# Four attention-fed MLPs on one core: three late matmul stages by a seven-product scheme on half tiles

## The chip, the cores and the metric

The kernel runs on 1 core of one Trainium2 chip. The metric is the device time of one execution in microseconds (us). The program is built by a scheduler that reorders the instructions of each engine, so the order on an engine is not the order of the source.

## The reference, cut to what matters

```python
# attention: 4 batches x 12 heads, 448 x 64, float32; all MLP weights float64
q_n, k_n = rmsnorm(q, g_q), rmsnorm(k, g_k)
attn = softmax(scale * q_n @ k_n.T)              # per batch and head
x = (attn @ v)  ->  [1792, 768]                  # 4 batches x 448 tokens
ab = (x @ w_a) * (x @ w_b)                       # w_a, w_b: 768 x 1536
y = ab @ w_out                                   # 1536 x 768
h = y @ w2_in                                    # 768 x 2048
g = max(h, 0) + alpha * min(h, 0)
out = g @ w2_out                                 # 2048 x 768
```

## The kernel before, in words

**Tiles.** A batch b (448 tokens) is one pass through four stages: `a` gives AB[b, 0..11] (gated products), `y` gives Y[b, 0..5], `h` gives G[b, 0..15], `o` gives the output columns. Data lie transposed: 128 features on the partitions, 448 tokens along the free axis. Every float32 value is kept as two float16 values, high and low. A product of one 128x128 weight block with one 128x448 data tile is three matmuls into one PSUM bank (`prod`, L752, `mm`, L107): high by high, high by low, low by high. A *unit* is one weight tile's worth of these: 18 matmuls in `a`, `y` and `h` (six blocks), 12 in `o` (four blocks). A stage `a` has 24 units, `y` 12, `h` 16, `o` 24, that is 432, 216, 288 and 288 matmuls.

**Order.** `stages` (L594) sets the order of the stages, with the attention of later batches put between units at a rate that `RATE` (L920) sets; before `a` of batch b its attention is finished. Attention's PSUM pools (`ps_s`, two tiles of two banks, and `ps_x`, one bank) stay open to the end; the MLP stages use `ps_m` (three banks).

**Weights.** The first use of a weight tile loads it as float64, converts, scales and splits it on ACT and DVE (`w_convert`, `w_scale`, `w_split`), and writes the two float16 halves to HBM scratch (`sc_a`, `sc_y`, `sc_h`, `sc_o`). Every later use loads it from there (`w_load`, L618, DMA L624, on SP's queue) into one of 5 buffers (`wh_p`), asked for 4 units ahead (`AGAIN`, L720). `next_w` (L740) ends a unit: it drops the buffer, asks for loads, and takes one job from the list `tasks`.

**Ends of stages.** `stage_a` leaves AB in float32 (L788, DVE, with the sum of squares by ACT L791), then forms one scale for the batch from all twelve sums (`total` L123, a matmul named `tot` on TensorE, and `power` L110, four small DVE instructions, L797) and splits AB by it (`split`, L764), at once where `y` follows, else one tile a unit by `tasks`. `stage_o` finishes output chain m one chain behind: ACT scales and reorders (L880), TensorE transposes four 128x112 pieces (L887), ACT copies with a scale (L889), a DMA stores (L890).

**The end of a1** is where batch 2's attention, the last AB chain of batch 1 and y1 meet: DVE runs the softmax steps (L417 maximum, L472 and L473 sum and reciprocal, L480 the low half of the probabilities, L531 the low half of x) with the last AB chain (L788).

## Time and profile before

| | us |
|---|---|
| median of 3 runs (lowest, highest) | 1224.51 (1223.84, 1224.89) |
| the profiled execution | 1225.36 |
| its span in the trace | 1223.6 |
| TensorE (PE) busy | 1158.7 (95%) |
| VectorE (DVE) busy | 673.7 (55%) |
| ScalarE (ACT) busy | 714.4 (58%) |

PE's share is an average: in the first 340 us the weights are converted and the attention of batches 0 and 1 runs, and DVE, ACT and the DMA engines are as busy as PE; from a2 on (598 us to the end) DVE is busy for 172 of 626 us, and PE runs almost without a gap. The profile's own time is 0.85 us above the median, and its span is 1.76 us shorter than that time.

### The profile page before, as it was taken

Reading aid. Unit: us, or ns where it says so; the run is one execution under the profiler, and the core shown is the slowest. Engines: PE = TensorE matmul, PEld = TensorE weight load, DVE = VectorE, ACT = ScalarE, POOL = GpSimd, SP = SyncE. Lnnn points to the kernel's source line nnn. Section 1 sums busy time; section 2 is a strip of 40 time slices with the busy share of each in tenths; the row PEclk is TensorE's granted clock in tenths of the full one; section 3 lists DMA queues with packets and bytes.
Section 4 is the critical chain, followed back from the end, with each engine's and each line's share of the span. In section 5 each row is a group of like instructions: output and inputs, shape, how many; then the busy total and the mean of one; then the engine's idle time right before and its main releaser. Section 6 shows DMA issues by size and latency. Waiting matters only on the chain.

```text
span 1223.6 us, 18095 instructions
## 1 busy us (share of the span) xinstructions
PE 1158.7 (95%) x6550; PEld 595.6 (49%) x6550; DVE 673.7 (55%) x1442; ACT 714.4 (58%) x1458; POOL 11.9 (1%) x32
## 2 busy tenths in 40 slices
...
GB/s 186 175 164 217 311 324 324 278 298 301 318 261 300 266 257 246 189 230 177 208 153 126 168 106 168 192 191 163 104 116 116 116 117 107 105 151 128 95 129 88
DMA packets 311241, 234.65 MB, mean 192 GB/s; under 512 B 175440, under 2 KB 284496, under 8 KB 311152
## 3 DMA queue, kind: packets, MB, share of 16 engines
...
q0 software_dynamic: 112, 0.07, 0.1%
...
## 4 chain that ended last, share of the span: by engine, by line
PE 52%; DMA 1%; ACT 1%; DVE 1%; issue 0%; SPq 0%; ACTq 0%
PE p L108 48%; PE s L108 2%; PE x L108 2%; PE p L887 1%; DMA pT<-p 1%; DMA kr<-in_k_dram 0%; ACT t L880 0%; DMA qT<-q 0%; ACT pf L434 0%; ACT p L479 0%; DVE p L480 0%; DVE nm L417 0%; SPq L486 0%; DVE ab L788 0%; ACT x L530 0%
## 5 line engine op out<-in xcount | busy, mean ns | idle before, releaser
L108 PEld LDWEIGHTS <-w 128*128 128x128 f16 x4896 | 474.9, 99 | 466.9 <-issue 39.9
L108 PE MATMUL p<-x,w 128*128 128x448 f16 x1728 | 336.6, 354 | 0.3 <-DVE ab L788 0.2
L108 PE MATMUL p<-g,w 128*128 128x448 f16 x1152 | 228.1, 354 | 6.3 <-ACT g L847 2.2
L108 PE MATMUL p<-y,w 128*128 128x448 f16 x1152 | 222.3, 353 | 0.2 <-DVE t L862 0.2
L108 PE MATMUL p<-ab,w 128*128 128x448 f16 x864 | 169.5, 356 | 1.4 <-ACT ab L766 1.2
L417 DVE TENSOR_REDUCE nm<-s 128x2 f32<-128x896 f32 x84 | 91.2, 1085 | 38.3 <-PE s L108 38.2
L480 DVE SCALAR_TENSOR_TENSOR p<-pf,ri,p 128x448 f16<-128x448 f32 x126 | 84.1, 680 | 30.7 <-ACT p L479 30.5
L479 ACT ACTIVATE p<-pf,ri 128x448 f16<-128x448 f32 x126 | 81.2, 664 | 33.9 <-DMA pT<-p 25.8
L862 DVE SCALAR_TENSOR_TENSOR t<-t,al,p 128x448 f32<-128x448 f32 x55 | 37.3, 678 | 100.6 <-ACT t L861 100.5
L434 ACT ACTIVATE pf<-s,nm,esc 128x448 f32<-128x448 f32 x126 | 90.1, 719 | 1.4
L788 DVE SCALAR_TENSOR_TENSOR ab<-p,inv_a,t 128x448 f32<-128x448 f32 x48 | 32.5, 678 | 100.0 <-PE p L108 99.8
L880 ACT ACTIVATE t<-p,inv_o 128x448 f32<-128x448 f32 x24 | 25.6, 1065 | 81.5 <-PE p L108 81.5
L712 DVE SCALAR_TENSOR_TENSOR w<-wf,sc,w 128x768 f16<-128x768 f32 (+1 forms) x76 | 70.1, 928 | 3.0 <-ACT w L711 2.5
L791 ACT ACTIVATE junk<-ab 128x448 bf16<-128x448 f32 x48 | 27.6, 575 | 70.4 <-DVE ab L788 69.8
L711 ACT ACTIVATE w<-wf,sc 128x768 f16<-128x768 f32 (+1 forms) x76 | 65.5, 869 | 3.4 <-DMA sc_h<-w 1.7
L644 ACT ACTIVATE wf<-raw 128x768 f32<-128x768 f32 (+1 forms) x76 | 63.7, 843 | 4.6 <-DMA raw<-in_moe_w_in_dram 2.7
L650 DVE SCALAR_TENSOR_TENSOR wf<-raw,wf 128x768 int32<-128x768 int32 (+1 forms) x76 | 65.8, 867 | 0.3
L658 ACT ACTIVATE junk<-wf 128x768 bf16<-128x768 f32 (+1 forms) x76 | 59.2, 779 | 1.4 <-DVE wf L650 1.3
L861 ACT ACTIVATE t<-p 128x448 f32<-128x448 f32 x55 | 29.8, 542 | 48.0 <-PE p L108 47.9
L108 PE MATMUL s<-kT,qT 128*64 128x448 f16 x252 | 48.4, 376 | 9.2 <-DMA kT<-k 6.3
L847 ACT ACTIVATE g<-t,cgf 128x448 f16<-128x448 f32 x55 | 36.7, 668 | 34.6 <-DVE t L862 34.6
L848 DVE SCALAR_TENSOR_TENSOR g<-t,cgf,g 128x448 f16<-128x448 f32 x55 | 37.5, 682 | 29.5 <-ACT g L847 29.5
...
## 6 DMA issues: line engine op xcount, KB each, us to landing
w<-sc_a SPq DMA_DIRECT2D x72, 384.0 KB, 3.2
w<-sc_h SPq DMA_DIRECT2D x48, 384.0 KB, 3.1
w<-sc_o SPq DMA_DIRECT2D x72, 256.0 KB, 3.1
w<-sc_y SPq DMA_DIRECT2D x36, 384.0 KB, 3.2
...
```

The source lines that it names most:

```text
L108: nc.tensor.matmul(out=o, lhsT=a, rhs=b, start=first, stop=last)
L417: nc.vector.tensor_reduce(out=nm, in_=ps[:, :, 0:S], axis=AX.X, op=ALU.max, negate=True)
L434: nc.scalar.activation(out=pf, in_=ps[:, j, 0:S], func=AF.Exp, bias=nm[:, j:j + 1], scale=scale[j], accum_out=su[:, j:j + 1],)
L479: nc.scalar.activation(out=t[:, 0, :, 0:KP], in_=pf, func=AF.Copy, scale=r)
L480: nc.vector.scalar_tensor_tensor(out=t[:, 1, :, 0:KP], in0=pf, scalar=r, in1=t[:, 0, :, 0:KP], op0=ALU.mult, op1=ALU.subtract,)
L644: nc.scalar.activation(out=t, in_=hi.bitcast(F32), func=AF.Prelu, scale=2.0 ** -112, alpha=-(2.0 ** 32))
L650: nc.vector.scalar_tensor_tensor(out=ti, in0=lo, scalar=29, in1=ti, op0=ALU.logical_shift_right, op1=ALU.bitwise_or)
L658: nc.scalar.activation(out=junk(768, size(kind)), in_=t, func=AF.Square, accum_out=sums[0][:, j:j + 1])
L711: nc.scalar.activation(out=w[:, 0], in_=t, func=AF.Copy, scale=s)
L712: nc.vector.scalar_tensor_tensor(out=w[:, 1], in0=t, scalar=s, in1=w[:, 0], op0=ALU.mult, op1=ALU.subtract)
L848: nc.vector.scalar_tensor_tensor(out=x[:, 1], in0=t, scalar=cgf[:, f:f + 1], in1=x[:, 0], op0=ALU.mult, op1=ALU.subtract,)
L862: nc.vector.scalar_tensor_tensor(out=t, in0=t, scalar=al[:, f:f + 1], in1=ps, op0=ALU.mult, op1=ALU.add)
```

## The change

`stages` becomes "a0 y0 h0 o0 a1 y1 a2 h1 o1 y2 h2 a3 o2 y3 o2 h3 o3": h2 goes ahead of a3, and o2 is done in two pieces, its first two pairs of output chains ahead of y3 and the third behind it. Stages o2, y3 and o3 (`FAST`) use Strassen's scheme in Winograd's form: for a pair of output chains and for the two halves of the contraction and of the tokens, seven products of half tiles take the place of eight. A product has 128x128 weights and 128x224 data, and is again three matmuls. A pair takes 7 units of 18 matmuls in y (378 in the stage) and 14 units of 12 in o (504 in the stage). What comes with it:

- Four of the seven weight operands are sums of weight blocks (S1 to S4). `form_block` makes them from the scratch: 4 loads, one DVE add of the halves (L679), four DVE sums of a quarter each (L683 to L686), ACT's high half (L690), DVE's low half (L691), 4 stores. There are 12 such blocks for o (1024 elements a partition) and 6 for y (1536). They are written in the source from a2 on, one step a unit, as the list `back`.
- The data operands are sums too: `forms` (DVE L884 to L886 on 448, 224 and 224 elements, ACT L902 and DVE L904 or L906 for the halves, 1568 elements a partition in all) in `stage_h` of batches 2 and 3 and behind a3.
- Seven products of a pair are put together by `gather` (DVE adds out of PSUM, one ACT copy).
- The attention pools are closed ahead of h2, and their room goes to five PSUM banks (`ps_l`) and to the new tiles.
- Weights of fast units come from the scratch or from the formed sums into `wf_p` (6 buffers), still asked for 4 units ahead.
- The batch scale of AB (`scale`) is done at once where y follows, else two units into the next stage. Behind o2's pieces, transposes and stores go into the next stage's units by `tasks`; behind o3 they come one after the other.
- y takes AB's even tiles first, o its weight parts in the order 0, 2, 1, 3, and the powers of two of the scales move (`head`).

```diff
-    stages = "a0 y0 h0 o0 a1 y1 a2 h1 o1 y2 a3 h2 y3 o2 h3 o3".split()
+    stages = "a0 y0 h0 o0 a1 y1 a2 h1 o1 y2 h2 a3 o2 y3 o2 h3 o3".split()
+    FAST = ("o2", "y3", "o3")
+    OPEN = "h2"
+    PIECES = {"o2": [range(2), range(2, 3)]}
...
+    FORMS = (("A11", 0), ("S2", 5), ("S3", 2), ("A22", 6), ("S1", 1), ("S4", 4), ("A12", 3))
...
+    def form_block(kind, i, j, cols):
+        w = cols.stop - cols.start
...
+        def whole():
+            d["r"] = raw().bitcast(F32)[:, 0:4 * w].rearrange("p (q n) -> p q n", q=4)
+            nc.vector.tensor_tensor(d["r"], d["x"][:, :, 0, :], d["x"][:, :, 1, :], op=ALU.add)
+
+        def sums():
+            r = d["r"]
+            nc.vector.tensor_tensor(r[:, 3], r[:, 2], r[:, 3], op=ALU.add)
+            nc.vector.tensor_tensor(r[:, 2], r[:, 0], r[:, 2], op=ALU.subtract)
+            nc.vector.tensor_tensor(r[:, 0], r[:, 3], r[:, 0], op=ALU.subtract)
+            nc.vector.tensor_tensor(r[:, 1], r[:, 1], r[:, 0], op=ALU.subtract)
+
+        def halves():
+            d["o"] = o = raw().bitcast(F16)[:, 0:8 * w].rearrange("p (q l n) -> p q l n", q=4, l=2)
+            nc.scalar.copy(o[:, :, 0, :], d["r"])
+            nc.vector.tensor_tensor(o[:, :, 1, :], d["r"], o[:, :, 0, :], op=ALU.subtract)
+
+        def store():
+            for q, name in enumerate(("S2", "S4", "S3", "S1")):
+                nc.sync.dma_start(out=formed[kind, i, name, j][:, :, cols], in_=d["o"][:, q])
+
+        back.extend((load, whole, sums, halves, store))
...
+        if key[-1] == "s":
+            kind, i, (f, j), _ = key
+            t = wf_p.tile([128, 768], F32, tag="wf", name="ws").bitcast(F16)
+            t = t[:, 0:2 * WIDE[kind]].rearrange("p (l n) -> p l n", l=2)
+            nc.sync.dma_start(out=t, in_=form_source(kind, i, f, j))
+            w16[u] = t
+            return
...
+        elif back and cur[0] > state["back"]:
+            t = back.pop(0)
+            if t:
+                t()
...
+    def forms(r, s, name):
+
+        nc.vector.tensor_tensor(r[:, 1:3], r[:, 2:5:2], r[:, 0:3:2], op=ALU.subtract)
+        nc.vector.tensor_tensor(r[:, 5], r[:, 4], r[:, 1], op=ALU.subtract)
+        nc.vector.tensor_tensor(r[:, 6], r[:, 3], r[:, 5], op=ALU.subtract)
...
+        f = []
+        for j0, j1, x in parts:
+            nc.scalar.activation(out=x[:, 0], in_=r[:, j0:j1], func=AF.Copy, scale=s)
+            if s == 1.0:
+                nc.vector.tensor_tensor(x[:, 1], r[:, j0:j1], x[:, 0], op=ALU.subtract)
...
+    def fast(kind, F, pairs, evac):
...
+            for _ in range(7 * (last + 1)):
+                yield
+                u = cur[0]
+                _, _, (f, j), _ = stream[u]
+                w = unit()
...
+                ps = out[f]
+                for x in range(kk):
+                    hi, lo = w[:, 0, x, :], w[:, 1, x, :]
+                    t = F[j * kk + x][FORMS[f][1]]
+                    mm(ps, hi, t[:, 0], j + x == 0, False)
+                    mm(ps, hi, t[:, 1], False, False)
+                    mm(ps, lo, t[:, 0], False, j == last and x == kk - 1)
+                if j == last:
+                    evac(i, f, ps, None if apart else banks[BANKS[f][0]])
+                next_w()
...
+    def gather(d, f, ps, bank):
...
+        if f == 0:
+            d["p"], d["u"] = pair(), pair()
+            nc.scalar.copy(d["p"][:, 0], ps)
+        elif f == 1:
+            add(d["p"][:, 1], ps, d["p"][:, 0])
+        elif f == 2:
+            add(d["u"][:, 0], ps, d["p"][:, 1])
...
+                x, add_to = 0, d.pop("p")
+            if bank is None:
...
+            else:
+                d[x] = late["t"].tile([128, S], F32, tag="t", name="t2")
+                add(halves_of(d[x]), halves_of(bank[:, 0:S]), add_to)
+            if f == 4:
+                add(d["p"][:, 1], ps, d["p"][:, 1])
...
+    def fast_o(b, pairs):
...
+        d, ready, turned = {}, [], []
+
+        def evac(i, f, ps, bank):
+            if f in (1, 6) and turned:
+                turn_out(b, *turned.pop(0))
+            if f in (0, 5) and ready:
+                m, t, s = ready.pop(0)
+                turned.append((m, turn_in(t, s)))
+            gather(d, f, ps, bank)
+            for j, at in ((1, 4), (0, 6)):
+                if f == at:
+                    m = 2 * i + j
+                    ready.append((m, d.pop(j), inv["o"][:, m:m + 1]))
+
...
+        else:
+            for m, t, s in ready:
+                tasks[0:0] = [
+                    lambda t=t, s=s: turned.append(turn_in(t, s)),
+                    lambda m=m: turn_out(b, m, turned.pop(0)),
+                ]
...
-        power(total(ssab[:, b % 2], KF), sab[:, b:b + 1], iab[:, b:b + 1])
+
+        def scale():
+            power(total(ssab[:, b % 2], KF), sab[:, b:b + 1], iab[:, b:b + 1], 2)
+
+        now = stages_after("a", b) == "y"
+        after(now, lambda f: f and f(), [scale] if now else [None, scale])
...
+        def pair(i):
+            r, at = blocks()
+            for j in range(2):
+                nc.scalar.copy(at[j], halves_of(raw.pop(2 * i + j)))
+            AB[b, i] = forms(r, sab[:, b:b + 1], f"ab{b}_{i}")
+
+        if f"y{b}" in FAST:
+            for i in range(KF // 2):
+                tasks.extend((lambda i=i: pair(i), None, None, None))
...
+            if f"o{b}" in FAST:
+                i, j = f // 2, f % 2
+                if j == 0:
+                    rs[i] = blocks()
+                nc.scalar.activation(
+                    out=rs[i][1][j], in_=halves_of(t), func=AF.Copy, scale=cgf[:, f:f + 1]
+                )
+                if j == 1:
+                    G[b, i] = forms(rs.pop(i)[0], 1.0, f"g{b}_{i}")
+                return
...
+            if st == "a2":
+                for kind in "oy":
+                    for x in range(CHAINS[kind][0] // 2):
+                        form_weights(kind, x)
+                state["back"] = cur[0]
+            if st == OPEN:
...
+                att_ctx.close()
+                late["ps"] = ctx.enter_context(
+                    tc.tile_pool(name="ps_l", bufs=5, space=bass.MemoryType.PSUM)
+                )
+                late["f"] = ctx.enter_context(tc.tile_pool(name="lf", bufs=8))
+                late["q"] = ctx.enter_context(tc.tile_pool(name="lq", bufs=3))
+                late["t"] = ctx.enter_context(tc.tile_pool(name="lt", bufs=4))
```

On **DVE at the end of a1** stood, before (x_3 is a tile of batch 2's attention, `ab_1_11` the last AB chain of batch 1):

```order
L480 SCALAR_TENSOR_TENSOR p_2_110<-pf,ri,p_2_110 128x4x112
L417 TENSOR_REDUCE nm<-s 128x2
L480 SCALAR_TENSOR_TENSOR p_3_111<-pf,ri,p_3_111 128x4x112
L472 TENSOR_SCALAR su<-su 128x2
L473 RECIPROCAL ri<-su 128x2
L531 SCALAR_TENSOR_TENSOR x_3_6390<-x,x_3_6390 128x448
L386 SCALAR_TENSOR_TENSOR v_6745<-vr,sx,v_6745 112x8x64
L480 SCALAR_TENSOR_TENSOR p_0_108<-pf,ri,p_0_108 128x4x112
L788 SCALAR_TENSOR_TENSOR ab_1_11_6414<-p,inv_a,t 128x448
```

and now (line numbers are the changed kernel's, so L480 is L484, L472 is L476, L531 is L535 and L788 is L1051; `raw` is a tile of `form_block`):

```order
L679 TENSOR_TENSOR raw<-raw 128x1024
L476 TENSOR_SCALAR su<-su 128x2
L683 TENSOR_TENSOR raw<-raw 128x256
L477 RECIPROCAL ri<-su 128x2
L684 TENSOR_TENSOR raw<-raw 128x256
L685 TENSOR_TENSOR raw<-raw 128x256
L686 TENSOR_TENSOR raw<-raw 128x256
L691 TENSOR_TENSOR raw<-raw 128x4x256
L535 SCALAR_TENSOR_TENSOR x_3_6393<-x,x_3_6393 128x448
L390 SCALAR_TENSOR_TENSOR v_6748<-vr,sx,v_6748 112x8x64
L484 SCALAR_TENSOR_TENSOR p_0_111<-pf,ri,p_0_111 128x4x112
L1051 SCALAR_TENSOR_TENSOR ab_1_11_6417<-p,inv_a,t 128x448
```

The third of the weight blocks that the scheduler has brought forward into a1 stands between p_3 and x_3; two more are earlier in a1, three in y1, and six of o's with one of y's in a2; the rest of y's are in h2 and a3.

On **PE at the start of h1** (`w_7695` is the weight tile of its first unit before, `w_7840` and `w_7867` those of its second and third now, `tot<-ssab` the sum for AB's scale of batch 2) stood, before:

```order
L108 LDWEIGHTS w_7695
L108 MATMUL p<-y_3_6849,w_7695 128x448
L108 MATMUL tot<-ssab,ones 128x12
L108 LDWEIGHTS w_7695
L108 MATMUL p<-y_3_6849,w_7695 128x448
```

and now:

```order
L110 LDWEIGHTS w_7840
L110 MATMUL p<-y_5_7055,w_7840 128x448
L110 MATMUL tot<-ssab,ones 128x12
L110 LDWEIGHTS w_7867
L110 MATMUL p<-y_0_6546,w_7867 128x448
```

The matmul for the scale has moved from the middle of the first unit to the boundary of the second and third.

On **ACT at the end of the program** (`t` scaled chains of o3, `ob` the copies that are stored, `q_..<-l` the first product of the last pair) stood, before:

```order
L880 ACTIVATE t_12022<-p_11942,inv_o_139 128x7x64
L889 ACTIVATE ob_12029<-p_12024,cum_135 112x512
L880 ACTIVATE t_12089<-p_12009,inv_o_139 128x7x64
L889 ACTIVATE ob_12096<-p_12091,cum_135 112x512
L880 ACTIVATE t_12135<-p_12076,inv_o_139 128x7x64
L889 ACTIVATE ob_12142<-p_12137,cum_135 112x512
```

and now:

```order
L1167 ACTIVATE t_13243<-t2_13212,inv_o_142 128x7x64
L963 COPY q_13245<-l_13216 128x224
L1180 ACTIVATE ob_13282<-p_13277,cum_138 112x512
L1167 ACTIVATE t_13403<-t2_13373,inv_o_142 128x7x64
L1180 ACTIVATE ob_13434<-p_13429,cum_138 112x512
L1167 ACTIVATE t_13439<-t2_13437,inv_o_142 128x7x64
L1180 ACTIVATE ob_13446<-p_13441,cum_138 112x512
```

Before, `t` and `ob` take turns, chain by chain, with a chain of matmuls between them; now the last two `t` stand behind the last pair's products, with one `ob` between them, and on PE the last eight transposes stand together at the end.

## Rows read from the trace of the kernel before

**Rows 1.** The page's section 1, PE: busy time, share of the span, instructions.

```profile
PE 1158.7 (95%) x6550; PEld 595.6 (49%) x6550; DVE 673.7 (55%) x1442; ACT 714.4 (58%) x1458; POOL 11.9 (1%) x32
```

**Rows 2.** Stage windows of PE (o0, y1, y3, o3): length, busy (instructions), clock, DMA share, GB/s.

```profile
338.00:431.70 93.70, 78.38 (x463) 0.98 1.09 273
...
547.20:597.70 50.50, 50.50 (x301) 0.99 0.81 189
...
1006.70:1047.60 40.90, 40.90 (x218) 1.00 0.35 103
...
1160.50:1223.60 63.10, 57.52 (x314) 0.98 0.38 106
```

**Rows 3.** PE's waits: 600 to 760 us, from 1000 us, 538 to 548 us.

```profile
PE tot L108 <- ACT junk L791: 1.8, 1, 1.8
...
PE p L887 <- ACT t L880: 2.3, 2, 1.1
...
PE tot L108 <- ACT junk L791: 3.3, 1, 3.3
```

**Rows 4.** The timeline's end: start, length, engine, line, operation, tiles, [idle before, releaser].

```profile
1209.96 0.60 PE L887 MATMUL p<-ident,t 128*112 128x128 f32 x4
...
1210.40 6.97 PE L108 MATMUL p<-g,w 128*128 128x448 f16 x36
...
1217.41 1.06 ACT L880 ACTIVATE t<-p,inv_o 128x448 f32<-128x448 f32 x1 [6.07 <-PE p L108]
...
1218.52 0.65 PE L887 MATMUL p<-ident,t 128*112 128x128 f32 x4 [1.15 <-ACT t L880]
1219.26 0.69 ACT L889 ACTIVATE ob<-p,cum 112x512 f32<-112x512 f32 x1 [0.79 <-PE p L887]
```

**Rows 5.** Groups by shape, PE's weight loads: busy, mean ns, idle before, releaser.

```profile
L108 PEld LDWEIGHTS <-w 128*128 128x128 f16 x4896 | 474.9, 99 | 466.9 <-issue 39.9 <-ACT w L711 3.9 <-DVE w L712 1.3
...
L887 PEld LDWEIGHTS p<-ident,t 128*112 128x112 f32 x96 | 11.2, 134 | 10.6 <-ACT t L880 8.0
```

**Rows 6.** Groups by shape, DVE and ACT durations of 448 to 768 elements.

```profile
L711 ACT ACTIVATE w<-wf,sc 128x768 f16<-128x768 f32 x52 | 48.9, 942 | 3.4 <-DMA sc_h<-w 1.7 <-PE p L108 1.5
...
L711 ACT ACTIVATE w<-wf,sc 128x512 f16<-128x512 f32 x24 | 16.6, 713 | 0.0
...
L352 DVE TENSOR_TENSOR k<-kr,k 112x512 f16<-112x512 f32 x18 | 12.3, 684 | 1.1 <-ACT k L343 1.1
...
L326 DVE TENSOR_TENSOR qr<-qr,r 128x448 f32<-128x448 f32 x18 | 11.2, 620 | 0.1
```

**Rows 7.** DVE's timeline at a1's end and, last, at y1's end.

```profile
539.14 0.17 DVE L472 TENSOR_SCALAR su<-su 128x2 f32<-128x2 f32 x1 [1.33 <-ACT pf L434]
...
540.10 0.62 DVE L531 SCALAR_TENSOR_TENSOR x<-x,x 128x448 f16<-128x448 f32 x1 [0.59 <-ACT x L530]
...
541.97 0.68 DVE L788 SCALAR_TENSOR_TENSOR ab<-p,inv_a,t 128x448 f32<-128x448 f32 x1
...
596.77 0.62 DVE L531 SCALAR_TENSOR_TENSOR x<-x,x 128x448 f16<-128x448 f32 x1
```

**Rows 8.** Stage windows of DVE (y1, h2), columns as in rows 2.

```profile
547.20:597.70 50.50, 37.03 (x80) 0.99 0.81 189
...
951.90:1006.70 54.80, 28.92 (x47) 1.00 0.39 116
```

**Rows 9.** DMA view: queue share and issues in o1, then in 220 to 330 us.

```profile
q1 hardware_dynamic: 26129, 13.02, 75.4%
...
w<-sc_o SPq DMA_DIRECT2D x21, 256.0 KB, 3.2
...
sc_h<-w SPq DMA_DIRECT2D x14, 384.0 KB, 7.5
```

**Rows 10.** The view of tile w on SP's queue, from 950 us to the end.

```profile
DMA to landing us min/median/max: 2.8/3.0/4.8
```

More of the change, by code (lines that the diff above doesn't have):

```diff
@@ new lines, in units_of, with chains, form_source @@
+    def units_of(st, i):
+        if st[0] == "y":
+            return [(f, 0) for f in range(7)]
+        if st == "o3" and i == 0:
+            return [(f, j) for j in range(2) for f in range(7)]
+        return [(f, j) for f in range(7) for j in range(2)]
+    WIDE = {"y": 768, "o": 512}
+    def chains(kind, i):
+        return (2 * i, 2 * i + 1)
+    def form_source(kind, i, f, j):
+        name = FORMS[f][0]
+        if name[0] == "S":
+            return formed[kind, i, name, j]
+        n = chains(kind, i)[int(name[1]) - 1]
+        two = int(name[2]) - 1
+        return scratch[kind, n, two if kind == "y" else 2 * two + j]
@@ L702, in junk @@
     def junk(width, n):
[L703 removed]
+        return jk_p.tile([128, width], BF16, tag="junk", name="junk")[:, 0:n]
     def w_split(u):
@@ L722, in attention_gated_mlps_kernel @@
     seen = set()
-    firsts = [u for u, key in enumerate(stream) if not (key in seen or seen.add(key))]
+    firsts = [u for u, key in enumerate(stream) if key[-1] != "s" and not (key in seen or seen.add(key))]
     again = sorted(set(range(len(stream))) - set(firsts))
@@ L806, in stages_after, with after @@
         return stages[i + 1][0] if i + 1 < len(stages) and stages[i + 1][1] == str(b) else ""
-    def after(now, one, n):
+    def after(now, one, each):
         if now:
-            for i in range(n):
+            for i in each:
                 one(i)
         else:
-            tasks.extend((lambda i=i: one(i)) for i in range(n))
+            tasks.extend((lambda i=i: one(i)) for i in each)
     def stage_y(b):
```

257 lines of the change are left out of this document (195 added, 62 removed).

## The prediction, made before the changed kernel ran

> **What bounds the kernel now.** I read the page's busy times first, then the windows of the stages, then PE's waits, then the timelines at the places that the change touches. PE is busy for 95% of the span [rows 1]; the windows show where the rest is. The stages that change, y3 and o3, run at full clock with PE busy for 40.90 of 40.90 and 57.52 of 63.10 us, the latter cut only by the tail [rows 2]; the DMA engines have a share of 0.35 to 0.38 there. So late in the program the time is the number of matmuls by their pitch: y3 is 12 units of 18, 40.90 / 216 = 189.4 ns for a matmul of 448 columns. Early it is otherwise: o0 has 15.3 us without PE in 93.70, at a DMA share of 1.09. The change takes matmuls out where only PE counts, and puts DVE and DMA work (the weight sums) into a1, y1 and a2, where the attention of the next batch is also on DVE. The first is the gain, the second the price.
>
> **The change part by part.** All is set against the profiled execution, 1225.36 us.
>
> *The products.* y3, o2 and o3 have 216 + 288 + 288 = 792 matmuls of 448 columns now: 792 x 189.4 = 150.0 us. Afterwards there are 378 + 504 + 504 = 1386 of 224 columns. No matmul of 224 columns of this kind stands in the trace, so I bound it. At 2.4 GHz, the level of these stages [rows 2], 448 columns are 186.7 ns, and 2.7 of the 189.4 are left over. From below: half of all, 94.7 ns, 131.3 us, -18.7. From above: the four transposes of 128 columns, whose next matmul starts 0.44 us after the first of them [rows 4], 110 ns each, 152.5 us, +2.5. I take 93.3 + 2.7 = 96.0 ns, 133.1 us, **-16.9**: the left-over once per matmul, near the lower end, because a 448-column matmul is the same instruction with the same weight load, while the transposes are of f32 with loads of 134 ns against 99 ns [rows 5]. That 99 ns is itself longer than 96.0, and could be the new floor: 1386 x 99 = 137.2, -12.8; I hold it for a record that overlaps its neighbours, but it belongs in the range.
>
> The Trainium skill, page "TensorE: Matmul & The Clock Gate", section "LDWEIGHTS (loading the stationary operand)", gives a weight load the time of its columns over 1.2, in ns; for 128 columns that is 107 ns (an estimate from that page), and if the load then set the pitch, 1386 of them would be 148.3 us and the gain 1.7 instead of 16.9. The f16 loads of this trace are recorded at 99 ns, 7% shorter, so it is too slow for this case as it stands; that loads bound the pitch at all is rival C.
>
> *The wait for AB's scale.* PE stands 1.8 us in h1's first unit for the sum of squares that ACT has yet to end [rows 3]. `tot` now stands two units on, over 6 us later: **-1.8** (between that and 0). At a1's end, where y1 follows at once, the like wait of 3.3 us stays.
>
> *Ends of o2 and o3.* Both wait for L880 ahead of the last transposes, 2.3 us together [rows 3]. Behind o2 the transposes now go into units of the next stage, so half of it goes: **-1.1** (to 0). At the very end it gets longer. Now the last matmul is followed by ACT's scaling (1.06), the transposes, ACT's copy (0.69) and the store [rows 4]. Afterwards a DVE addition of 448 elements out of PSUM (0.62 by the like row [rows 6], and some 0.06 of hand-over) comes first, and the copy and transposes of two chains share the end, of which up to 0.69 + 0.5 us can show: I take **+1.2** (0.7 to 1.9).
>
> *The weight sums: their size.* DVE takes 172 ns + 1.0 ns an element (620 at 448, 684 at 512) and ACT 713 ns at 512 and 0.894 more an element [rows 6]. A block for o is 1.2 (1024) + 4 x 0.43 (256) + 1.2 = 4.1 us of DVE, 1.17 of ACT; for y (1536 and 384) 5.6 of DVE. The scheduler puts three into a1, three into y1, seven into a2, five later.
>
> *At a1's end.* The third block stands on DVE between p_3 and x_3, ahead of the last AB chain, whose sum of squares y1's start waits for. DVE idles there for 1.33 us until 539.14 and 0.59 until 540.10 [rows 7]. The first addition (1.2) fits into the first gap. Then come the four sums, 1.72 us, to about 541.15 with the two small softmax steps between; then ACT's half, 1.17 and a hand-over, to 542.4; then DVE's half, 1.2, to 543.7; then x (0.62), v, p and ab as before (ab began 1.87 after x [rows 7]), so that ab ends near 546.3 instead of 542.65: **+3.6**. It is on the path, for all of y1 needs that scale, and PE was already waiting for it. From 0 (other work of PE moves into it) to 5 (a late load too).
>
> *In y1.* Three blocks, 12.3 us, into a stage where DVE is idle for 50.50 - 37.03 = 13.5 us [rows 8], in pieces. The chain that matters is batch 2's attention: its last tile ends at 597.39 [rows 7], and a2's first unit (from 597.70) needs it after 15 of 18 matmuls, 2.8 us on: 3.1 us to spare. If all fits, 0; if nothing fits, 12.3 - 3.1 = 9.2. I take one block of the three as not fitting, 4.1 - 3.1 = **+1.0**, near the lower end, because PE waits for nothing in y1 now (50.50 of 50.50 [rows 2]).
>
> *At nothing.* In a2 seven blocks (30 us) and in h2 the data sums and two y blocks come to a DVE with room: h2 has 28.9 us of 54.8 now [rows 8], and gets 8 x 1.8 (0.62 + 0.40 + 0.40 + 1.74 less two splits of 0.68) + 2 x 5.6 = 25.6 more, 54.5 in all, just full; but PE waits only for the emptying of PSUM, which stands ahead of the sums, and o2 comes a whole a3 later. If that cover is gone, the excess is at most the last pair, 3 us. In o3 the first pair's units go by the first half of the contraction, so that late G sums are hidden behind seven units of 1.15 us. Weight loads: a fast unit of o has 12 x 96.0 = 1.15 us, 256 KB for it; with 6 buffers a load is asked for five units ahead, 5.75 us, against 3.2 us to landing at a queue share of 75% [rows 9] and 4.8 at the worst late in the program [rows 10].
>
> *The sum:* -16.9 - 1.8 - 1.1 + 1.2 + 3.6 + 1.0 = -14.0; 1225.36 - 14.0 = 1211.36. The profiled execution lies 0.85 above the median, so 1210.5 on the median.
>
> **The rivals.**
>
> *A, the forecast:* 1210.5, by itself 1207 to 1214.5 (the upper end has the pitch of 99 ns).
>
> *B, the early losses are hidden:* other work slides into a1's end and the y1 blocks fit. Without 3.6 and 1.0: 1205.9. For it speaks that y1 has as much idle DVE time as the blocks want; against it that the third block stands ahead of the awaited chain in DVE's own order.
>
> *C, slower: the pitch does not halve.* A half tile needs a weight load for half as many columns; if loads of 128 columns, not columns of data, set the pace, there are 594 more of them than before. The other terms sum to +2.9, so it decides from (150.0 - 2.9) / 1386 = 106.1 ns on. At the 110 ns of the transposes [rows 4]: +2.5 + 2.9 = +5.4, 1229.9. Against it: the f16 load's 99 ns [rows 5] is below 106.1; for it: that no matmul under 448 columns shows in these stages.
>
> *D, the attention slips in y1:* DVE and DMA so full that PE has gaps as in o0, 15.3 of 93.70 or 16% [rows 2]; 16% of y1 is 8.2 us instead of 1.0: 1217.7. For it: a1 and o0 run at a DMA share around 1, and the blocks add loads and stores to them. Against it: PE's full y1.
>
> *E, late weights:* landing takes over 5.75 less 0.5 of issue, about 5.2 us. At the 7.5 us of a full queue [rows 9] a unit would last (7.5 + 0.5 + 1.15) / 6 = 1.53 us instead of 1.15, and over the 84 units of o2 and o3 that is +32: 1242. Against it: o1's 3.2 us.
>
> **How the numbers follow.** A 0.58, B 0.15, D 0.13, C 0.08, E 0.04, and 0.02 for more of a1's loss than D has, still under the time before. A measurement of this kernel can tell about 0.2% (2.4 us) from no change. A, B, D and the remainder are faster by more than that: 0.88. C spreads around its break-even: half of it, 0.04, is the same, the other half with E slower, 0.08. The range holds A, B and D and the 99 ns: 1205 to 1219; C and E are left out.
>
> **What would show it.** Matmuls of 128x224 that follow each other by 96 ns in o2, y3 and o3 (99 or 107 to 110 would be C); PE's wait for `tot` at a1's end at about 7 us instead of 3.3, and none in h1; waits of PE for x or for probabilities at y1's end and in a2 below 2 us (over 7 is D); L959's last addition, then L1167, eight transposes and one L1180 behind the last product, some 1.2 us longer than now; w's landing near 3.2 us in o2 and o3 (over 5.2 is E); DVE nearly full in h2 with PE not waiting. The forecast is wrong above all if the pitch is not 96: each ns on it is 1.39 us.

## The result

The changed kernel takes 1239.14 us (median of 4 runs, 1231.94 to 1240.62) against 1224.7 for the kernel before: 1.0103 times its time, 95% interval 1.0078 to 1.0129. It is slower by about 14 us; 1210.5 was forecast, and the range ended at 1219. The profiled execution is one of 1237.92 us, its span 1236.0.

The stages of the changed kernel, PE's windows (start and end in us; then length, busy (instructions), granted clock, DMA share, GB/s), that answer to [rows 2]:

```profile
434.70:559.00 124.30, 110.33 (x660) 0.95 1.05 245
559.00:610.90 51.90, 51.90 (x300) 0.96 0.91 225
610.90:713.30 102.40, 92.50 (x490) 0.97 0.83 220
...
893.30:954.10 60.80, 55.21 (x290) 1.00 0.55 170
...
1036.60:1080.00 43.40, 43.40 (x453) 1.00 0.83 251
...
1178.40:1236.00 57.60, 51.26 (x529) 0.97 0.64 189
```

These are a1, y1, a2, h2, the first half of the stretch of o2 and y3, and o3. The windows of a1, a2 and h2 before, columns as above:

```profile
431.70:547.20 115.50, 110.33 (x660) 0.98 1.00 231
...
597.70:686.20 88.50, 88.27 (x489) 1.00 0.58 151
...
951.90:1006.70 54.80, 54.77 (x291) 1.00 0.39 116
```

The late stages do what was meant: o2, y3 and o3 together take 144.5 us instead of 162.3. The loss is early: a1 124.2 us (115.5 before), a2 102.4 (88.5), h2 60.9 (54.9). Of a2's 13.9 us, 9.7 are time in which PE runs no matmul (9.9 us now, 0.2 before); the other 4.2 are busy time, in a stage whose granted clock is 0.97 instead of 1.00.

The fast stages' matmuls in PE's timeline, and the end of the program, that answers to [rows 4]:

```profile
1053.28 4.76 PE L110 MATMUL l<-g,ws 128*128 128x224 f16 x48
```

```profile
1221.80 6.78 PE L110 MATMUL l<-g,ws 128*128 128x224 f16 x69
...
1228.61 0.62 DVE L959 TENSOR_TENSOR t<-l,q 128x448 f32<-128x448 f32 x1 [3.68 <-PE l L110]
...
1230.82 0.65 PE L1178 MATMUL p<-ident,t 128*112 128x128 f32 x4 [1.81 <-ACT t L1167]
1231.56 0.69 ACT L1180 ACTIVATE ob<-p,cum 112x512 f32<-112x512 f32 x1 [0.79 <-ACT t L1167]
```

48 matmuls in 4.76 us, the last of them recorded with 0.26: 4.50 / 47 = 95.7 ns each, as forecast (96.0). From the last product's end to the span's end it is 7.4 us, 6.2 before: +1.2, as forecast.

What a2 waits for. First SP's queue (total, times, longest), before and after:

```profile
SPq L624 <- PE p L108: 53.3, 18, 4.0
```

```profile
SPq L695 <- DVE raw L691: 10.9, 5, 6.5
SPq L726 <- PE p L110: 7.5, 4, 4.2
```

Before, SP stood idle for 53 of 88.5 us until PE gave a weight buffer back; it was ahead of its work. Now that slack is 7.5 us, and SP stands 10.9 us before the store of a weight sum (L695) that DVE has not finished (L691), with the next loads behind it. Added up over the DMAs that it issues, SP is busy for some 73 of 102.4 us in a2 (27 of 88.5 before) and for some 106 of 124.2 in a1 (87 of 115.5); a load or store of a block takes about 0.6 us of it (median 0.61 in a2), eight a block. One such place, from all engines' timeline:

```profile
694.49 0.66 SPq L675 DMA_DIRECT2D raw<-sc_y  x1
695.25 0.55 SPq L726 DMA_DIRECT2D w<-sc_a  x1
695.89 1.28 SPq L355 DMA_TRANSPOSE qT<-q  x1
...
698.81 1.76 DVE L679 TENSOR_TENSOR raw<-raw 128x1536 f32<-128x1536 f16 x1 [5.88 <-DMA raw<-sc_y]
...
701.67 0.68 DVE L1051 SCALAR_TENSOR_TENSOR ab<-p,inv_a,t 128x448 f32<-128x448 f32 x1
...
702.40 2.15 PE L110 MATMUL p<-x,w 128*128 128x448 f16 x7 [3.45 <-DVE ab L1051]
```

The last load of a block of y is issued at 694.49, 6.0 us behind the third one, with four stores of another block between them. DVE waits 5.88 us for it, and everything that DVE has to do behind it waits too, among it L1051, which empties the PSUM bank that PE wants: PE stands 3.45 us. A gap of 2.75 us at 639.58 comes by a longer way: the load of k for the attention is issued at 633.59, behind a block's stores and the attention's transposes; ACT waits 5.4 us for it, DVE's L240 5.9 us for ACT, and L1051 stands behind L240. In h2 the instruction that empties PSUM is L1150. It stands on DVE behind the additions of y's two blocks and of the data sums, and is PE's only wait there (`PE p L110 <- DVE t L1150`, 5.6 us in 5 pieces); the data sums alone cost nothing in h2 (54.5 us in e2 below). At a1's end the wait for `tot` is 6.8 us instead of 3.3 [rows 3].

### The profile page after: what moved, and what is told of

Same layout as the page of the kernel before. It is cut to its first block, busy times and chain, and to the rows that moved or that the text cites. A ratio compares the mean times of both kernels' runs of the same rounds, so it can differ in the third digit from the quotient of the medians.

```text
span 1236.0 us, 19915 instructions
## 1 busy us (share of the span) xinstructions
PE 1148.2 (93%) x7144; PEld 652.2 (53%) x7144; DVE 810.9 (66%) x1659; ACT 767.7 (62%) x1525; POOL 12.4 (1%) x32
## 5 line engine op out<-in xcount | busy, mean ns | idle before, releaser
L110 PEld LDWEIGHTS <-w 128*128 128x128 f16 x4104 | 399.4, 99 | 415.8 <-issue 63.5
L110 PE MATMUL p<-x,w 128*128 128x448 f16 x1728 | 340.1, 356 | 12.9 <-DVE ab L1051 6.1
L110 PE MATMUL p<-y,w 128*128 128x448 f16 x1152 | 222.3, 352 | 6.4 <-DVE t L1150 6.4
L110 PEld LDWEIGHTS <-ws 128*128 128x128 f16 x1386 | 132.9, 98 | 0.5
L110 PE MATMUL p<-ab,w 128*128 128x448 f16 x648 | 131.9, 364 | 1.2 <-ACT ab L874 1.2
L110 PE MATMUL p<-g,w 128*128 128x448 f16 x576 | 118.3, 359 | 4.6 <-ACT g L1135 3.5
L421 DVE TENSOR_REDUCE nm<-s 128x2 f32<-128x896 f32 x84 | 91.2, 1086 | 27.3 <-PE s L110 27.2
L484 DVE SCALAR_TENSOR_TENSOR p<-pf,ri,p 128x448 f16<-128x448 f32 x126 | 84.1, 680 | 30.7 <-ACT p L483 30.6
L110 PE MATMUL l<-g,ws 128*128 128x224 f16 x960 | 93.8, 259 | 0.0
L438 ACT ACTIVATE pf<-s,nm,esc 128x448 f32<-128x448 f32 x126 | 90.3, 722 | 1.4
L1054 ACT ACTIVATE junk<-ab 128x448 bf16<-128x448 f32 x48 | 27.8, 579 | 57.2 <-DVE ab L1051 57.2
L110 PE MATMUL s<-kT,qT 128*64 128x448 f16 x252 | 48.5, 376 | 11.3 <-DMA kT<-k 6.0
L1051 DVE SCALAR_TENSOR_TENSOR ab<-p,inv_a,t 128x448 f32<-128x448 f32 x48 | 32.5, 677 | 37.4 <-PE p L110 37.4
L110 PE MATMUL s<-kT,qS 128*64 128x448 f16 x252 | 46.9, 366 | 2.6 <-DMA qS<-qT 2.6
L110 PE MATMUL s<-early 128*128 128x448 f32 x84 | 39.7, 599 | 9.9 <-ACT pf L438 9.3
L1150 DVE SCALAR_TENSOR_TENSOR t<-t,al,p 128x448 f32<-128x448 f32 x55 | 36.6, 676 | 15.5 <-ACT t L1149 15.5
```

Of the source, the lines that this page charges most:

```text
L110: nc.tensor.matmul(out=o, lhsT=a, rhs=b, start=first, stop=last)
L421: nc.vector.tensor_reduce(out=nm, in_=ps[:, :, 0:S], axis=AX.X, op=ALU.max, negate=True)
L438: nc.scalar.activation(out=pf, in_=ps[:, j, 0:S], func=AF.Exp, bias=nm[:, j:j + 1], scale=scale[j], accum_out=su[:, j:j + 1],)
L484: nc.vector.scalar_tensor_tensor(out=t[:, 1, :, 0:KP], in0=pf, scalar=r, in1=t[:, 0, :, 0:KP], op0=ALU.mult, op1=ALU.subtract,)
L1051: nc.vector.scalar_tensor_tensor(out=ab, in0=ps, scalar=i, in1=t, op0=ALU.mult, op1=ALU.mult)
L1150: nc.vector.scalar_tensor_tensor(out=t, in0=t, scalar=al[:, f:f + 1], in1=ps, op0=ALU.mult, op1=ALU.add)
```

## The experiments

18 kernels. Ratios are to the kernel before, run beside each, with 95% intervals. The table has the stages of each profiled execution, in us, from a stage's first matmul to the next stage's; o0 and a1 differ by several us between kernels that have the same work there, the others hardly.

| kernel | us | o0 | a1 | y1 | a2 | o1 | y2 | h2 | a3 | o2+y3 | o3 |
|---|---|---|---|---|---|---|---|---|---|---|---|
| before | 1224.7 | 93.7 | 115.5 | 50.5 | 88.5 | 71.4 | 46.9 | 54.9 | 81.7 | 99.3 | 63.0 |
| the change | 1239.1 | 95.9 | 124.2 | 51.9 | 102.4 | 71.1 | 46.8 | 60.9 | 82.3 | 86.9 | 57.6 |
| e1 sums late | 1236.2 | 98.5 | 118.4 | 52.0 | 88.1 | 90.3 | 55.8 | 54.5 | 82.0 | 86.9 | 57.6 |
| e2 no sums | 1210.1 | 97.7 | 118.8 | 52.1 | 88.1 | 71.5 | 46.8 | 54.5 | 81.7 | 86.9 | 57.6 |
| e3 plain order | 1230.7 | 96.1 | 116.4 | 51.0 | 88.8 | 71.7 | 46.9 | 54.5 | 85.2 | 100.8 | 63.1 |
| e4 sums pinned | 1234.4 | 97.3 | 119.8 | 51.1 | 97.5 | 83.2 | 47.8 | 55.0 | 82.5 | 86.9 | 57.6 |
| e5 GpSimd's queue | 1230.4 | 102.3 | 117.8 | 50.9 | 88.1 | 84.9 | 47.6 | 54.5 | 84.2 | 86.9 | 57.6 |
| e6 math only | 1216.7 | 97.7 | 119.4 | 50.7 | 88.7 | 78.2 | 46.8 | 54.5 | 81.7 | 86.9 | 57.9 |
| e7 DMAs only | 1242.8 | 96.4 | 134.4 | 51.4 | 88.5 | 89.3 | 46.8 | 54.5 | 82.0 | 86.9 | 57.6 |
| e8 all in a3 | 1271.1 | 95.0 | 118.7 | 50.8 | 88.5 | 71.6 | 46.8 | 54.5 | 84.6 | 146.1 | 57.7 |
| e9 spread | 1240.5 | 96.0 | 118.6 | 51.6 | 88.2 | 71.4 | 46.8 | 54.5 | 90.4 | 106.8 | 58.1 |
| e10 y3 and o3 | 1227.3 | 99.9 | 120.3 | 50.6 | 88.1 | 71.2 | 46.8 | 57.0 | 84.0 | 98.6 | 57.6 |
| e11 tiny DMAs | 1236.6 | 95.5 | 130.3 | 50.6 | 88.1 | 85.7 | 46.8 | 54.5 | 81.7 | 86.9 | 57.6 |
| e12 plain, G's order | 1231.6 | 100.7 | 114.8 | 51.6 | 88.1 | 71.9 | 46.8 | 54.5 | 85.2 | 101.1 | 63.1 |
| e13 y3 alone | 1225.0 | 96.7 | 120.8 | 51.8 | 88.2 | 71.4 | 46.8 | 54.6 | 81.8 | 94.7 | 62.9 |
| e14 two DMAs | 1228.8 | 95.2 | 119.8 | 51.7 | 88.9 | 89.2 | 47.8 | 54.5 | 81.7 | 86.9 | 57.8 |
| e15 two DMAs, spread | 1212.8 | 97.2 | 117.1 | 50.7 | 88.2 | 71.3 | 46.8 | 54.5 | 81.7 | 92.7 | 57.4 |
| e16 loads ahead | 1227.3 | 99.7 | 120.1 | 51.4 | 88.8 | 85.8 | 46.9 | 54.5 | 81.7 | 86.9 | 57.4 |
| e17 e15, loads ahead | 1217.2 | 95.6 | 119.7 | 50.9 | 88.7 | 71.2 | 46.8 | 54.5 | 81.7 | 92.6 | 57.4 |
| e18 only two DMAs | 1232.7 | 96.0 | 128.8 | 54.0 | 96.4 | 71.4 | 46.8 | 56.6 | 81.7 | 86.9 | 57.5 |

### Which part of the change costs it: e1 to e4

e1 writes the sums later and pins their first DVE addition to its place in the program; e4 only pins it.

```diff
-            nc.vector.tensor_tensor(d["r"], d["x"][:, :, 0, :], d["x"][:, :, 1, :], op=ALU.add)
+            tc.keep_in_program_order(
+                nc.vector.tensor_tensor(d["r"], d["x"][:, :, 0, :], d["x"][:, :, 1, :], op=ALU.add)
+            )
...
-            if st == "a2":
-                for kind in "oy":
+            for kind in [k for k, at_ in (("o", "o1"), ("y", "a3")) if st == at_]:
```

> The whole change, with the weight sums moved: those for o are written from o1 on and those for y from a3 on, two steps a unit, and the first DVE addition of each block keeps its place in the program, so that no block stands on DVE before h1's end and at most one in h2. Theory (the early place of the sums on DVE costs a1, a2 and h2 about 29 us together): a1, y1, a2 and h2 fall back to their times before, 115.5, 50.5, 88.5 and 55, the late gain of 18 us stays: 1204 to 1211 us. Rival 1 (the new stage order and the pools closed early cost it): h2 and a2 stay long, 1225 or more. Rival 2 (the 35 MB of added DMA traffic costs it wherever it runs): 1225 or more, the loss now in o1, y2 and a3.

Measured 1236.24, 1.0089 (1.0064 to 1.0115). a2 and h2 fall back as expected (a1 only to 118.4), but o1 and y2, where eleven of o's twelve blocks now stand beside batch 3's attention, take 27.8 us more than without sums (e2); a3 takes y's six blocks for nothing. The loss moved with the blocks: not the early place as such, but, so far, the company of attention.

e2 leaves the blocks out; a sum's unit reads a scratch tile:

```diff
-        if name[0] == "S":
-            return formed[kind, i, name, j]
-        n = chains(kind, i)[int(name[1]) - 1]
+        n = chains(kind, i)[int(name[1]) % 2 if name[0] == "S" else int(name[1]) - 1]
...
```

> The changed kernel without the weight sums: the blocks are left out, and the fast units read a weight tile of the scratch in the place of each sum. Theory: all of the early loss is the blocks, 1203 to 1209 us, a1 115.5, a2 88.5, h2 near 55. Rival 1 (stage order and pools): 1220 or more, a2 and h2 still long. Rival 2 (DMA traffic of the blocks): as the theory here, told apart by the run with late sums.

1210.11, 0.9873 (0.9844 to 0.9903), just above what was expected, with a1 at 118.8 instead of 115.5. So the blocks cost the change 29 us, and without them the rest is a gain of 15.6 us.

e3 has no fast stage (`FAST = ()`), no blocks, o2 in one piece behind y3.

> The changed kernel with no fast stage and no sums: products as before, but the new order (h2 ahead of a3), the pools closed at h2, the scale of AB two units late, the parts of y and o in the new order. Theory: nothing of the loss is here, 1221 to 1225 us (the kernel before less up to 3 us of waits). Rival 1: 1230 to 1240 us.

1230.68, 1.0041 (1.0022 to 1.006): 5 us slower than before, outside what was expected. a3 (+3.5) and o2 with y3 (+1.5) are peculiar to it and to e12; o0 and a1 are longer in nearly the whole family of kernels made from the change (below).

> The changed kernel with one edit: the first DVE addition of each weight block keeps its place in the program, so that none stands in a1, one at y1's end, five in a2 and h1, six in o1, the others in y2, h2 and a3. Theory: a1 and y1 fall back by 8 to 10 us, a2 by 3 to 8, h2 stays long or gets longer since one more of y's blocks is there: 1220 to 1230 us. Rival 1 and rival 2 (stage order, DMA traffic): as the changed kernel, 1235 to 1241 us.

1234.43, 1.0073 (1.0046 to 1.01), beyond the theory's end: a2 falls back by 5 us and h2 by 6 (h2 was expected to stay long), but o1, which has five of the blocks now, takes 83.2. As in e1, the loss goes where blocks meet attention.

### What of a block costs it: e5 to e7, e11

All four are e1 with something taken away; e7 and e11 pin a block's first store in place of its first addition.

e5: `nc.sync.dma_start` becomes `nc.gpsimd.dma_start` in a block's load and store.

> The kernel with late sums (o's in o1 and y2, y's in a3), but the loads and stores of the blocks are issued by GpSimd, whose queue is nearly empty, not by SP. In the run with late sums o1 took 90.3 us and y2 55.8, without sums 71.5 and 46.9; SP was issuing for 81 of 90 us there, against 39 of 71 before. Theory (the blocks' eight DMAs each, some 0.63 us of issue apiece, fill SP's queue, and the transposes and loads of the attention behind them come late): o1 under 77, y2 under 50, in all 1210 to 1218 us. Rival D (DVE's work and its order): o1 85 or more, 1230 to 1238. Rival B (the DMA engines' bandwidth, share 0.90 in that stage): likewise 1230 or more.

1230.4, 1.0039 (1.001 to 1.0068). y2 falls back (47.6), o1 only from 90.3 to 84.9: half of the 27.8 us goes with the issues off SP's queue, with the same DVE work and about the same bytes (20.2 MB in o1, 20.7 in e1). That lies between the theory (o1 under 77) and its rivals. The edit isn't a clean one: from GpSimd the bytes go in fewer packets (28936 in o1, 41164 in e1). The Trainium skill, page "DMA: Bandwidth & Descriptors", section "Rules for kernel authors", says that spreading DMAs over the issuing engines doesn't help bandwidth and only saves the sequencer's issue time. That agrees with this run: 13.6 us come back though the DMA share of o1 rises, 0.90 to 0.95.

e6: no loads, no stores, the arithmetic on a tile that is set once.

> The kernel with late sums, its blocks without their loads and stores: the same DVE and ACT instructions on a tile that is set once, at the same places; the fast units read scratch tiles in the place of the sums. Theory (SP's queue): o1 71 to 77 us, y2 47 to 49, 1209 to 1216 in all. Rival D (DVE's work): o1 83 or more, 1225 or more.

1216.69, 0.9937 (0.9908 to 0.9966): o1 78.2 (71 to 77 was expected), 6.7 us over e2's; y2 loses nothing.

e7: the loads and stores alone.

```diff
         def whole():
-            d["r"] = raw().bitcast(F32)[:, 0:4 * w].rearrange("p (q n) -> p q n", q=4)
-            nc.vector.tensor_tensor(d["r"], d["x"][:, :, 0, :], d["x"][:, :, 1, :], op=ALU.add)
+            d["o"] = d["x"]
...
+        halves = sums
```

> The kernel with late sums, its blocks without arithmetic: the four loads and the four stores of each stay on SP's queue, the store takes the loaded tile as it is, so the values of the sums are left out. Theory (SP's queue): most of the loss of o1 and y2 stays, o1 83 or more, y2 51 or more, 1224 to 1236 us. Rival D (DVE's work): o1 under 76, 1208 to 1216 us. Rival B (bandwidth): as the theory here; told apart by the run with GpSimd's queue.

1242.79, 1.0137 (1.0103 to 1.0171): o1 89.3, nearly all of e1's loss there, without an instruction on DVE. The scheduler also brought five blocks' loads into a1, and a1 grew to 134.4; y2, which has few of the DMAs left, takes 46.8 where 51 or more was expected.

e11 is e7 with 8 columns a block: `cols = slice(cols.start, cols.start + 8)`.

> The run with the blocks' DMAs alone, each DMA cut to 8 columns of its block (4 KB instead of 128 or 192 KB), as many DMAs at the same places of SP's order; no arithmetic, the fast units read scratch tiles. In the run with full DMAs a1 took 134.4 us and o1 89.3; without sums 118.8 and 71.5. Theory (SP's issue of eight DMAs a block): a1 128 or more, o1 83 or more. Rival B (bytes through the DMA engines): a1 under 121, o1 under 75.

1236.63, 1.0107 (1.0077 to 1.0137): a1 130.3 and o1 85.7. With a thirty-second of the bytes, 11.5 of 15.6 us stay in a1 and 14.2 of 17.8 in o1 (over e2). Neither the bytes nor the number of packets explains it: e11's o1 has 40102 packets, as many as e7's (39440), and the queue's share of the DMA engines is 75.8%, as without sums (76.2% in e2). SP waits 1.0 us in it for the blocks' landings and issues for 73 of 85.7 us (39 of 71.5 in e2): what is left is the issues. How they reach PE, in e1's o1 (window, then ACT's and PE's waits, then the timeline):

```profile
753.40:843.70 90.30, 74.87 (x426) 0.94 0.90 229
```

```profile
ACT p L483 <- DMA pT<-p: 18.4, 6, 8.2
...
PE p L1179 <- ACT t L1168: 15.1, 5, 5.8
```

```profile
764.53 2.59 SPq L697 DMA_DIRECT2D f_o_S<-raw  x4
...
784.60 4.49 SPq L490 DMA_TRANSPOSE pT<-p  x3
...
788.60 0.67 ACT L483 ACTIVATE p<-pf,ri 128x448 f16<-128x448 f32 x1 [8.25 <-DMA pT<-p]
789.17 0.67 ACT L1181 ACTIVATE ob<-p,cum 112x512 f32<-112x512 f32 x1
```

The four stores of a block hold SP for 2.59 us. SP issues for 81 of the 90 us (38 of 71 before, added up as above), so the attention's transposes (pT, in order on the same queue) go out late; ACT's next softmax step waits 8.25 us for one, o's output steps (L1168, L1181) stand behind it on ACT, and PE waits 15.1 us for those. By ACT's order, two of these five waits of PE (10.1 us) follow on late transposes and two others (4.7 us) on a softmax maximum (L421) that DVE gave late. From issue to landing pT takes 3.8 us, 3.5 before: the time is lost ahead of the issue, not on the way.

### Where the sums could go: e8 to e10

e8: all blocks from a3 on, four steps a unit. e9: from h2 on, one step a unit, two in a3. e10: only y3 and o3 fast, in the order of before.

> The changed kernel with all weight sums in a3 and the start of o2, where no attention runs: four steps a unit from a3 on, o's first two pairs, y's, o's third pair, the first DVE addition of each block pinned. DVE has 74 of 82 us free there, SP 74. Theory: nothing waits for SP's queue there but weight loads that are asked for four units ahead; a3 82 to 86 us, 1207 to 1214 in all, the fastest of the correct versions. Rival D (DVE's work): a3 88 or more, for its emptying of PSUM stands behind blocks of 4 to 5.6 us; 1216 to 1225. Rival B: a3 85 or more as well, at a DMA share near 1.

1271.09, 1.0376 (1.0342 to 1.041). No attention runs there, yet the stage overflows: o2 and y3 take 146.1 us, with one gap of PE of 17.7 us before y3. PE waits there for y3's data (L903 on ACT), which stand behind the last three blocks, of o, on DVE and ACT. The last two of these begin 10.8 us apart on DVE: a block in that row lasts as long as its chain of load, additions, store and the next block's load behind that store on SP.

> The whole change, its weight sums spread over the stages in which no attention runs: one step a unit in h2, two in a3, one in o2, in the order o's first two pairs, y's, o's third pair; the first DVE addition of each block pinned. Three blocks stand in h2, eleven in a3, four in o2. Theory (the sums cost where they share SP's queue and DVE with the attention, and are nearly free elsewhere as long as a stage has room for them): a1, y1, a2, o1 and y2 as without sums (a2 88, o1 71.5, y2 47), h2 54 to 58, a3 82 to 85, o2 and y3 together 87 to 92 (86.9 in the changed kernel): 1211 to 1219 us. Rival (a block costs 2 us wherever it is, attention or not): 1240 or more. Against both: if the stages run out of room as in the run with all sums in a3, o2's weights come late again and o2 is longer than 60.

1240.53, 1.0122 (1.0096 to 1.0149): a1 to h2 as without sums, so the place is right, but a3, with nine blocks' additions, loses 8.7 us, and o2 with y3, with six, loses 19.9. PE's waits from a3 to y3:

```profile
PE p L110 <- DVE ab L1054: 6.6, 2, 4.4
PE p L110 <- ACT junk L1057: 5.1, 1, 5.1
PE l L110 <- DMA ws<-f_o_S: 4.5, 2, 2.3
```

The theory that blocks are free away from attention, as long as a stage has room on DVE, falls with these two: before, DVE is busy for 8 of 82 us in a3.

> Only y3 and o3 by seven products, o2 as before, the stages in the order of before, the pools closed at a3; y's sums in a3 (two steps a unit), o's in the rest of a3, h2, y3 and o2 (one a unit). Theory: no block meets the attention of a batch, and the matmuls of y3 and o3 fall from 504 of 448 columns to 882 of 224: 95.4 - 84.1 = 11.3 us of them, 2 lost again at the end and at edges: a3 82 to 83, h2 55 to 57, y3 36 to 37, o3 57.6; 1211 to 1217 us. Rival (2 us a block wherever it is): 1235 or more.

1227.27, 1.0013 (0.9992 to 1.0033): no difference. o3 is 5.4 shorter, but o2 with y3 only 0.7, h2 and a3 are 4.4 longer, and o0 and a1 11 longer.

### The number of DMAs: e14 to e18

e14 is e1 with the four weight tiles of a pair in one HBM tile, and the four sums in one, so that a block has one load and one store of the same bytes:

```diff
-                nc.sync.dma_start(out=x[:, q], in_=s)
+            nc.sync.dma_start(out=x, in_=quad[kind, i, j][:, :, :, cols])
...
+            nc.sync.dma_start(out=sums_of[kind, i, j][:, :, :, cols], in_=d["o"])
```

> The run with late sums (o's in o1 and y2, y's in a3) with one DMA for the four loads of a block and one for the four stores: the four weight tiles of a pair lie in one HBM tile, so do the four sums; the same bytes and pieces, a quarter of the issues. In the run with late sums o1 took 90.3 and y2 55.8, SP issuing for 81 of 90 us. Theory (SP's time goes by the number of DMAs): SP 50 us or less in o1, o1 78 to 82 (DVE's part, 6.7, stays), y2 47 to 49: 1218 to 1226. Rival S (SP's time goes by the pieces of a DMA): an issue lasts 2 us and more, o1 86 or more, 1230 to 1238. Rival B (bytes): likewise 1230 or more.

1228.77, 1.0022 (1.0006 to 1.0037). An issue of four times the bytes lasts about as long in o1 as one of the small ones (median 0.57 us, 0.54 to 0.97), and SP issues for 58 of 89 us instead of 81 of 90. That is less of a fall than the number alone would give, since the loads of o's weights beside them last longer (0.8 us on average, 0.6 in e1). y2 falls back to 47.8. But o1 stays at 89.2, which the theory had at 78 to 82. DVE's wait, the DMA queue's share and landings there:

```profile
DVE raw L678 <- DMA raw<-sc_o: 12.6, 6, 3.9
```

```profile
q1 hardware_dynamic: 43072, 22.17, 97.1%
...
raw<-sc_o SPq DMA_DIRECT2D x9, 512.0 KB, 5.7
```

> The run with two DMAs a block, sums late, with the load of each block written ahead of the block before it, so that a block's first addition finds its data. In the run with two DMAs o1 was still 89.2 us although SP issued for only 56 of 82 us; DVE waited 12.6 us for the blocks' loads there, the softmax maximum behind it and ACT behind that. Theory W (in o1 DVE's waits for the loads now stand in for SP's queue): o1 77 to 81, y2 47 to 48: 1216 to 1221 us. Rival B (bytes, DMA share 0.97 in o1): o1 86 or more, 1225 or more.

e16 (each load written ahead of the block before it): 1227.28, 1.0007 (0.9991 to 1.0022), o1 85.8. Theory W had 77 to 81. So in o1 issues, DVE's work and its waits for loads can each stand in for another. ACT's two large waits there show it: for transposes (pT) 7.6 us without sums (e2), 18.4 in e1, 4.7 in e14 and 16.5 in e16; for DVE's softmax maximum (L421) 11.8, 16.3, 19.3 and 9.9. How the 14 to 18 us divide among them, and with bytes (DMA share 1.04 there), stays open.

> The whole change with one load and one store a block, G split in o's order, and the sums written from y2 on: one step a unit, two in a3, so that four blocks stand in y2, three in h2, eight in a3, three in o2. Theory (SP's issues by number, and DVE's order, are what the sums cost): y2 47 to 50, h2 54 to 57, a3 82 to 86, o2 and y3 together 87 to 90: 1210 to 1218 us. Rival S: y2 52 or more, a3 88 or more, 1225 to 1240 as in the run with spread sums.

e15 is e9 with two DMAs a block, begun in y2 and with G's order of e12: 1212.75 (1209.81 to 1216.33), **0.989 (0.9869 to 0.9911)**, the fastest; 27.8 us under e9. a3 is 81.7 (e9: 90.4), o2 with y3 92.7 (106.8). SP issues for 31 of 82 us in a3, in e9 for 59 of 90. Three edits are in it; G's order gave nothing in e12. The start in y2 brings three blocks more ahead of o2 (15 of 18 by their first additions, 12 in e9), so the gain in o2 and y3 is not the DMAs' alone. a3 is the cleaner comparison: it has ten blocks in e15 and nine in e9, and loses nothing. PE's waits from a3 to y3, to be set against e9's:

```profile
PE l L110 <- DMA ws<-sc_o: 3.0, 3, 1.5
PE l L110 <- DMA ws<-f_o: 0.8, 1, 0.8
```

> The run with two DMAs, sums from y2 on (1212.8 us), with one edit: each load written ahead of the block before it. There the first piece of o2 took 38.5 us against 33.7 without sums, y3 37.8 against 36.7. Theory W: o2's first piece 34 to 37, 1208 to 1212 us. Rival (the stages are full, not waiting): 1212 to 1216.

e17: 1217.23, 0.9923 (0.9903 to 0.9943). o2's first piece is 36.3 instead of 38.5, as theory W had it, but y3 takes 39.8 instead of 37.8: nothing gained, and the time of the whole is above what W and its rival had, nearer the rival's.

> The changed kernel with one edit: a block's four loads are one DMA and its four stores are one, in tiles of HBM that hold four. Written from a2 on as in the change; the scheduler puts five blocks into a1, four into y1, four into a2. Theory (the number of issues is most of what a block costs in a1, y1 and a2): 1222 to 1232 us, a2 90 to 95, a1 118 to 124. Rival (DVE's place and the bytes): 1236 or more, a1 126 or more.

e18, the change as it was but for the number of DMAs: 1232.68, 1.006 (1.0039 to 1.0082). a2 96.4 and h2 56.6 instead of 102.4 and 60.9. By their first additions six blocks stand in a1 instead of three, and five in a2 instead of eight; a1 is longer (128.8), so a2's gain is in part a matter of place. Over the whole kernel the edit is worth 5 to 6.5 us (by the ratios, by the times) of the 29 that the blocks cost among attention. All else that a block brings stays, and how it divides is not shown.

### The five us that are left: e12, e13

> The run in plain order (no fast stage, no sums), with one edit: at the end of h0, h1, ... the tiles of G are split in the order in which o now takes them (0, 2, 4, 6, 1, 3, 5, 7, 8, ...), not 0 to 15. In every run of the changed kernel's family o0's PE waits 3.5 to 3.6 us for one such split near its start, before the change 2.2 in two pieces, and o0 is 94.9 to 102.3 us at a granted clock of 0.93 to 0.94, against 93.7 at 0.98 before. Theory G (the order of o's parts without that of G's splits costs o0 some 3 to 5 us): the wait 2 us or less, o0 93 to 95, 1224 to 1228 in all (the plain order 1230.7). Rival (the five us come from elsewhere, the moved pools or chance): the wait goes, 1229 or more stays.

e12 splits G's tiles at the end of h in o's order (`sorted(raw, key=lambda f: (f // 8, f % 2, f))`): 1231.56, 1.0044 (1.0029 to 1.0058), the wait of 3.6 us at o0's start unchanged. Theory G falls; by the code, most of the splits are done two a unit before that line is reached.

> Only y3 by seven products, its six sums in a3 (two steps a unit, pinned), the stages in the order of before, pools closed at a3, G split in o's order; o2 and o3 as before. Theory: the sums cost nothing in a3 (81.7 to 83), y3 36.7 to 38 instead of 40.9, h1 3.6 shorter by the late scale, and nothing new early if theory G holds: 1217 to 1222 us, faster than the kernel before. Rival (a block costs 2 us wherever it is): a3 93 or more. If theory G is wrong: 1222 to 1227.

1225.01, 0.9991 (0.9978 to 1.0004): a3 81.8 with y's sums, o2 with y3 4.6 shorter, h1 3.6 shorter, and as much lost early again (o0 3.0, a1 5.3). What the family loses in o0 and a1 stays open. A trace of it: PE's windows after o0's start, before and in e2. The granted clock of the window (1.00 is the 2.4 GHz level, 0.50 the 1.2 GHz one) is lower in e2, where PE stood for 3.5 us just before it, than before, where it stood for 1.9 and 1.0 us:

```profile
345.00:352.00 7.00, 5.82 (x27) 0.76 1.06 290
```

```profile
344.00:351.00 7.00, 6.95 (x23) 0.59 1.07 314
```

## Why the prediction was wrong

- **The products:** right. -16.9 was forecast, and PE's pitch is 95.7 ns; rival C (pitch above 106) is out. The load time of 107 ns for 128 columns, an estimate from the Trainium skill (page "TensorE: Matmul & The Clock Gate", section "LDWEIGHTS (loading the stationary operand)"), did not set the pace.
- **The waits for `tot` and at the end:** right in place. h1 is 3.6 us shorter where 1.8 was forecast, since the clock is 1.00 in it instead of 0.97; the end is 1.2 longer, as forecast. Together with the products the late stages gave 17.8.
- **At a1's end:** +3.6 forecast, the wait grew by 3.5. y1: +1.0 forecast, +1.4 measured, but that is no sign of the blocks, for e2 has 52.1 without them (by their first additions two blocks stood in y1, not three, and eight in a2, not seven). a1 lost 8.7 in all: 3.3 of it without blocks too (118.8 in e2), 3.5 by the wait, and the rest, about 2, by the blocks ahead of its end, which had no term.
- **The step that failed** is "at nothing": a2 lost 13.9 and h2 6.0. It priced a block as DVE and ACT work and looked for room on these. A block is also eight DMAs on SP's queue, 18 x 8 = 144 issues of 0.6 us or some 86 us of SP, whose slack in a2 the profile showed (53 us). The working priced DMAs only as the weight loads of o2 and o3, and named the blocks' loads and stores only in rival D. And its DVE sums were counted as busy time only: an addition whose load had not landed held up what stood behind it on DVE, the emptying of PSUM too, up to 5.9 us at a time. In h2 the working had that emptying ahead of the sums and DVE just full (54.5 us); it stood behind them, and PE waited 5.6 us for it although DVE was busy for only 40.0 of 60.9 us.
- **The size of the miss:** the blocks cost 29 us (e2), the working had 4.6. The range ended 20 us under the result because rival D, the one with the blocks' DMAs in it, was placed in y1 alone and priced by o0's gaps (7 us more); the loss was in a1, a2 and h2. Its reason, the blocks' loads and stores beside attention, is one that the runs bear out; in o1 the carrier was SP's issues, with the transposes behind them, and not a full DMA queue (e7, e11). In a1 and a2 of the change itself, how the loss divides between SP's queue and DVE's order is read from the trace and not parted by a run.
- **B and E:** B is out; E did not come: the weights landed in 3.4 us at the median, 5.2 at the most.
- **The rest:** without sums 1205.9 was forecast and 1210.1 measured; the family's loss in o0 and a1 (7.3 us in e2), less what h1 and the late stages gave beyond the forecast, about makes up the difference, and no run here explains that loss.
